# A two-stage kernel on one core: first rows for the MLP by a product with a 0/1 matrix, and the first units in another order

## The chip, the cores and the metric

The kernel runs on one core of one Trainium2 chip. The metric is the time of one execution in microseconds, measured on the device. Before the change three runs took 219.55, 219.83 and 222.78 us, a median of 219.83.

A core has five engines, each with its own instruction queue, that meet only at semaphores: PE (matrix products; PEld in the profile is the loading of its stationary operand), DVE (vector), ACT (scalar functions, copies), POOL and SP (SP here only starts transfers). Sixteen DMA engines move data between HBM and the on-chip memory. Products are accumulated in PSUM, eight banks of 512 f32 numbers for each of 128 partitions, which DVE and ACT must read ("evict") before a bank is used again.

## What is computed

Linear attention on 8 batches of 8 heads, 576 rows of 64, and then a "mixture of depths": in each batch 128 of 576 rows go through an MLP, and the others are passed on.

```python
q_s = exp(q - max(q, -1)); q_s /= sum(q_s, -1) + 1e-9      # over the 64 of a row
k_s = exp(k - max(k, 2));  k_s /= sum(k_s, 2) + 1e-9       # over the 576 rows
kv = einsum('bhsd,bhse->bhde', k_s, v)
x  = einsum('bhsd,bhde->bhse', q_s, kv)                    # heads side by side: (8, 576, 512)
scores = einsum('bsd,d->bs', x, w_gate)
for b in range(8):
    top = argpartition(-scores[b], 128)[:128]
    h = maximum(x[b, top] @ w1, 0)                         # 512 -> 1024
    out[b] = x[b]
    out[b, top] += sigmoid(scores[b, top])[:, None] * (h @ w2)   # 1024 -> 512
```

Everything is f32. Inputs are q, k, v (9.4 MB each), w1 and w2 (2.1 MB each); the output has 9.4 MB.

## The kernel before

**Units.** The attention is cut into 16 units: a batch and four of its eight heads. 576 rows lie on 128 partitions, five (R) on even partitions and four on odd ones, the fifth being padded. For each unit `u` the steps are:

- `load` (L92): k, v, q from HBM, two transfers each, started by SP's queue into one of three sets of buffers (`u % 3`), so a load waits until the unit three before has been read.
- `k_exp` (L193, ACT, one exponential over k), `q_exp` (L198, ACT, in halves `i` = 0 and 1), `v_copy` (L204, v beside a column of ones; by DVE, or by POOL for units 1 to 4).
- `kv_mm` (L207, PE): 20 products that add up `k^T v` with the sums of k in the last column. The trace counts 40, since each f32 product is two instructions. `kv_out` (L219): DVE takes reciprocals (L224), ACT copies kv to `kv_w` (L226), DVE makes a column that holds kv times the gate's weights (L228, L229).
- `q_t` (L231): PE transposes q's exponentials (L239), 10 for each half, and ACT evicts them with a scale (`qT`, L242).
- `x_mm` (L246, PE, L253): x, its sums and its score in one product. `x_out` (L259, DVE): reciprocal (L266), the scaled x into `xs` (L267), the scores of these heads into `sr` (L269). `x_store` (L271): SP writes x to HBM.

**Selection.** After both units of a batch: `score` (L280) sums the heads' scores and splits row numbers and scores into bf16 parts (POOL, L292, L294). `score_row` (L296): PE lays the scores along a row (L302), ACT evicts it in two copies (L305, L307). `compare` (L310, DVE, five times): counts for each row how many come before it, its rank. `pick` (L329): DVE compares ranks with slot numbers to a 0/1 matrix `hit` (L335), a small product on PE (L339) gives each slot its row's number, three reductions and a minimum on DVE (L343 to L345) make the index, and POOL gathers the chosen rows of x from HBM (L347, an indirect DMA into `xr`). `gate` (L352) takes the sigmoid.

**MLP.** `turn` (L362): PE transposes the gathered rows (L368), ACT copies them to `xT` (L370). `mlp1` (L373, L382) and `mlp2` (L388, L392) run in eight pieces each; after pieces 4 and 8 of `mlp1` ACT takes the ReLU (L385). `finish` (L395) scales, adds and scatters the rows by an indirect DMA (L400, L401).

**Order.** `tc.manual_schedule()` (L104): each engine runs its instructions in the order in which the code writes them, and a framework adds the semaphores; what waits holds up all that is behind it on its engine. A PSUM tile name (`tp`, `mm`, `x`) has two buffers, used in turn. Before the first unit PE runs 20 bf16 products on ones (L120). The first loop (L520, s = 0 to 3, `EARLY` = 4) does the first four units with `fill` products between (L502; work for nothing), and in the order of its code the first batch's `score` (s = 1) and `pick` (s = 2). After it come `gate` and `turn` of batch 0 (L567, L568). The second loop (L571, s = 4 to 19) weaves unit s with the MLP of the batch four units back, `pieces(n)` (L577) being the next n pieces: `mlp1` in even s, `mlp2` in odd. In it the next unit's `v_copy`, `k_exp` and `kv_mm` are written in step s (L593, L594, L607), and `turn` of the next batch stands after five of `mlp2`'s pieces that follow `pick` (L597, L610, L621, L623).

Of the kernel before, what the change touches and what calls it, by code (L numbers as in the profile page):

```python
# [8 lines left out]
F32 = mybir.dt.float32  # L9
# [8 lines left out]
def kernel(  # L18
# [36 lines left out]
    UP = 2.0 ** 24  # L55
    TINY = 2.0 ** -126
    NV = 5
    WARM = 20
    assert S == 64 * (R + N2) and D == 64 and DM == H * D and DM == 512 and H % 4 == 0
    assert 1 < capacity < S and KF == 8 and NQ == 2  # L60
    assert B * S <= 32 * 256
# [27 lines left out]
    LD = 3  # L89
    raw = {w: [const.tile([P, 4, R, D], F32, name=f"{w}{n}") for n in range(LD)] for w in "qkv"}  # L90

    def load(u, which, queue=nc.sync):  # L92
        b, qd = units[u]
        for what in which:
            src = {"q": q, "k": k, "v": v}[what]
            t = raw[what][u % LD]
            first = src[b, 4 * qd].offset
            for n, rows in ((1, N2), (0, R)):
                queue.dma_start(
                    out=t[n::2, :, :rows].rearrange("p h r d -> p h (r d)"),  # L100
                    in_=bass.AP(tensor=src.tensor, offset=first + n * R * D,
                                ap=[[9 * D, 64], [SD, 4], [1, rows * D]]))

    ctx.enter_context(tc.manual_schedule())  # L104
    for n in range(LD):
        for what in "kvq":
            (nc.vector if n == 0 else nc.gpsimd).memset(raw[what][n][:, :, N2], 0.0)
    load(0, "k")
    load(0, "v", nc.scalar)
    load(0, "q")  # L110
    load(1, "kvq")
    load(2, "kvq")

    ones_b = const.tile([P, 4 * P], BF16, name="ones_b")
# [1 line left out]
    w_ps = bank("tp", 2)  # L118
    for n in range(WARM):
        nc.tensor.matmul(out=w_ps, lhsT=ones_b[:, :P], rhs=ones_b, start=True, stop=True)  # L120

    wg = const.tile([P, NQ, 2, D], F32, name="wg")
    for h in range(2):
        nc.scalar.dma_start(out=wg[part(h)].rearrange("p a i d -> p (a i) d"),
                            in_=bass.AP(tensor=moe_w_gate.tensor, offset=moe_w_gate.offset + h * D,
                                        ap=[[0, 64], [2 * D, 2 * NQ], [1, D]]))
    warm = const.tile([P, 1], F32, name="warm")
    nc.scalar.activation(out=warm, in_=ones_b[:, :1], func=AF.Exp)
    w1 = const.tile([P, KD, F], F32, name="w1")
# [98 lines left out]
        nc.vector.tensor_mul(prod, kv[:, :, :D], wg[:, qd])  # L228
        nc.vector.reduce_sum(out=kw[:, :, D + 1], in_=prod, axis=AX.X)  # L229

    def q_t(u, i):  # L231

        if i == 0:
            st["qT", u] = at.tile([P, 2, R, 2, D], F32, tag="qT", name="qT")
        qe = st["qe", u] if i == 0 else st.pop(("qe", u))
        t_ps = ps.tile([P, 2, 512], F32, tag="x", name="x", bufs=2)
        for r in range(R):
            for a in range(2):
                nc.tensor.transpose(out=t_ps[:, a, r * 64:(r + 1) * 64],  # L239
                                    in_=qe[part(a), i, r].rearrange("p h d -> p (h d)"),  # L240
                                    identity=ident[part(a), part(a)])
        nc.scalar.activation(out=st["qT", u][:, i].rearrange("p r a c -> p a r c"),  # L242
                             in_=t_ps[:, :, :R * 64].rearrange("p a (r c) -> p a r c", r=R),
                             func=AF.Copy, scale=krec[:, u, i:i + 1])

    def x_mm(u, i):  # L246

# [8 lines left out]

    xs, sr = {}, {}

    def x_out(u, i):  # L259
        b, qd = units[u]  # L260
        if qd == 0 and i == 0:
            xs[b] = xp.tile([P, R, NQ, 2, 2, D], F32, tag="xs", name="xs")
            sr[b] = md.tile([P, NQ * 2, G], F32, tag="sr", name="sr")
        x = st.pop(("x", u, i))[:, :, :R * C].rearrange("p h (r c) -> p h r c", r=R)
        rec = qrec[:, u, i].rearrange("p (h r) -> p h r", h=2)
        nc.vector.reciprocal(out=rec, in_=x[:, :, :, D])  # L266
        nc.vector.tensor_mul(xs[b][:, :, qd, i].rearrange("p r h d -> p h r d"), x[:, :, :, :D],  # L267
                             rec.to_broadcast([P, 2, R, D]))
        nc.vector.tensor_mul(sr[b][:, 2 * qd + i].rearrange("p (h r) -> p h r", h=2), x[:, :, :, D + 1], rec)  # L269

    def x_store(u):  # L271
        b, qd = units[u]
# [20 lines left out]
            if c < NV - 1:  # L293
                nc.gpsimd.tensor_sub(left, raw_s if c == 2 else left, vals[:, b, :, c])  # L294

    def score_row(b):  # L296
        s = st["s", b]
        srow = md.tile([P, RP], F32, tag="srow", name="srow")
        for r0, r1 in ((0, N2), (N2, R)):
            t_ps = bank("tp", 2)  # L300
            for r in range(r0, r1):
                nc.tensor.transpose(out=t_ps[:, (r - r0) * P:(r - r0 + 1) * P],  # L302
                                    in_=s[:, r:r + 1].to_broadcast([P, P]), identity=ident)
            if r0 == 0:
                nc.scalar.copy(out=srow[:, :N2 * P], in_=t_ps)  # L305
            else:
                nc.scalar.copy(out=srow[:, N2 * P:], in_=t_ps[:, :P:2])  # L307
        st["srow", b] = srow
# [20 lines left out]
    def pick(b):  # L329
# [3 lines left out]
        for n, (k0, m) in enumerate(slots):  # L333
# [15 lines left out]
                in_offset=bass.IndirectOffsetOnAxis(ap=idx[:m, :1], axis=0))  # L349
            st["pick", b, n] = xr, no, idx  # L350

    def gate(b, n):  # L352
        m = slots[n][1]
        xr, no, idx = st["pick", b, n]
        g = sl.tile([P, 1], F32, tag="g", name="g")
        nc.scalar.activation(out=g[:m], in_=no[:m, 1:2], func=AF.Exp, scale=-1.0)  # L356
        nc.vector.tensor_scalar_add(g[:m], g[:m], 1.0)  # L357
        nc.vector.reciprocal(out=g[:m], in_=g[:m])  # L358
        st["pick", b, n] = xr, g, idx


    def turn(b, n):  # L362
        m = slots[n][1]
        xr = st["pick", b, n][0]
        xT = sl.tile([P, KD, P], F32, tag="xT", name="xT")
        t_ps = bank("mm", 2)
        for d in range(KD):
            nc.tensor.transpose(out=t_ps[:, d * m:(d + 1) * m], in_=xr[:m, d * P:(d + 1) * P],  # L368
                                identity=ident[:m, :m])
        nc.scalar.copy(out=xT[:, :, :m], in_=t_ps[:, :KD * m].rearrange("p (d c) -> p d c", d=KD))  # L370
        st["xT", b, n] = xT

# [146 lines left out]

    for s in range(EARLY):  # L520
        q_t(s, 0)
        q_t(s, 1)
        k_exp(s + 1)
        v_copy(s + 1, nc.gpsimd)
        fill(2)
        x_mm(s, 0)
        x_mm(s, 1)
        fill(2)
        if s == 2:
            kv_mm(s + 1)  # L530
            q_exp(s + 1, 0)
            fill(3)
            pick(0)
            x_out(s, 0)
            kv_out(s + 1)
            x_out(s, 1)
            x_store(s)
            q_exp(s + 1, 1)
        else:
            x_out(s, 0)  # L540
            x_out(s, 1)
            x_store(s)
            if s == 1:
                score(0)
            kv_mm(s + 1)
            q_exp(s + 1, 0)
            kv_out(s + 1)
            if s == 1:
                score_row(0)
                for r in range(R):  # L550
                    compare(0, r)
            q_exp(s + 1, 1)
            if s == 3:
                score(1)
        fill(2)
        if s == 0:
            load_w1(0)
            load_w1(1)
        elif s == 1:
            load_w1(2)  # L560
            load_w1(3)
            load(4, "kvq")
            load(5, "kvq")
        else:
            load_w2(s - 2)
            load(s + 4, "kvq")
    each(gate, 0)  # L567
    each(turn, 0)  # L568

    number = None  # L570
    for s in range(EARLY, NU + LAG):  # L571

        mlp_b, odd = divmod(s - LAG, 2)
        piece = mlp2 if odd else mlp1
        f_next = 0

        def pieces(n):  # L577
            nonlocal f_next
            for _ in range(n):
                each(piece, mlp_b, f_next)  # L580
                f_next += 1

        here = s < NU
        after = s + 1 < NU
        last = s == NU - 1
        ends = s // 2 if here and odd else None
        compared = s // 2 - 1 if here and not odd else None
        chosen = (s - 3) // 2 if here and odd else B - 1 if s == NU else None
        if here:
            q_t(s, 0)  # L590
            q_t(s, 1)
        if after:
            v_copy(s + 1)  # L593
            k_exp(s + 1)  # L594
        pieces(2)
        if chosen is not None:
            pick(chosen)  # L597
        if here:
            x_mm(s, 0)
            x_mm(s, 1)  # L600
            x_out(s, 0)
            x_out(s, 1)
            x_store(s)
        if last:
            score(ends)
        if after:
            kv_and_exp(s + 1)  # L607
        if s + 4 < NU:
            load(s + 4, "kvq")
        pieces(1)  # L610
        if last:
            compared = ends
        if compared is not None:
            score_row(compared)
            for r in range(R):
                compare(compared, r)
        if chosen is not None:
            each(gate, chosen)
        if ends is not None and not last:
            score(ends)  # L620
        pieces(4)  # L621
        if odd and mlp_b + 1 < B:
            each(turn, mlp_b + 1)  # L623
        pieces(1)
        if odd:
            each(finish, mlp_b)
        if s == NU:
            number = sums_in_range()
# [28 lines left out]
```

## Time and profile before

| | us |
|---|---|
| runs: lowest, median, highest | 219.55, 219.83, 222.78 |
| the profiled execution | 217.89 |
| its span (first to last instruction) | 216.0 |
| PE busy, weight loads | 197.5 (91%), 147.2 (68%) |
| DVE, ACT, POOL busy | 116.2 (54%), 88.6 (41%), 34.4 (16%) |
| first product of the MLP (L382) | 42.64 |
| ranks of batch 0 complete (last L315) | 31.67 |
| PE busy of 0 to 10, 10 to 20, 20 to 30, 30 to 40, 40 to 50 | 7.72, 7.36, 7.56, 7.66, 9.97 |
| DMA share in the same stretches | 0.71, 1.08, 1.07, 1.06, 1.08 |

The profile is one execution, recorded by the hardware. Its page gives busy times, 40 slices of the span with each engine's busy share in tenths, the DMA queues, the chain of work that ended last, and the costliest groups of instructions. The trace answers for single instructions: start, duration, engine, line, what it writes and reads, and in brackets how long its engine sat idle before it and what ended that; "issue" means that the profile shows nothing that the engine waited for. A unit's load is 1.77 MB; between 20 and 80 us the DMA engines move some 375 GB/s. q1 is SP's queue, q10 ACT's, q0 POOL's (gathers and scatters), q8 and q14 bring instructions to the engines.

### The profile page before, as it was taken

To read this page: it belongs to the slowest core of one execution; us is meant where nothing else is said; L and a number is where in the kernel's file an instruction comes from. 1 tells how busy PE (TensorE), PEld (TensorE's weight loads), DVE (VectorE), ACT (ScalarE), POOL (GpSimd) and SP (SyncE) were. 2 spreads that over 40 slices of the span, in tenths; PEclk is the share of its full clock that TensorE was granted. 3 is DMA by queue.
4 is the path that set the end of the run, shared out by engine and by line. 5 is a ranking of instruction groups with operands and counts; after the bars stand their busy time and mean duration, and the time that the engine had idled before them with its cause. 6 is when DMAs were issued, how large, how long until landed. Compare 5 with 4: busy or idle time off the path is not lost. (4 is left out here: it accounts for less than half of the span.)

```text
span 216.0 us, 7090 instructions
## 1 busy us (share of the span) xinstructions
PE 197.5 (91%) x3040; PEld 147.2 (68%) x3040; DVE 116.2 (54%) x359; ACT 88.6 (41%) x146; POOL 34.4 (16%) x78
## 2 busy tenths in 40 slices
PE   5987595999999999999999999999999989999960
PEld 2464462799749975897679776996599548749620
DVE  6552595668726774477626872596358665501010
ACT  2386374763626471746265443536263311211100
POOL 6022402300112012200320023001120112101010
PEclk9999999999999999999999999999999999999996
DMA  5999999999999997958594949421313041101001
GB/s 179 299 356 358 375 398 369 362 392 377 377 384 381 375 344 249 314 157 283 171 320 154 313 133 303 161 82 49 113 52 109 7 156 52 49 3 52 5 5 52
DMA packets 39335, 46.81 MB, mean 217 GB/s; under 512 B 2944, under 2 KB 36736, under 8 KB 39296
## 3 DMA queue, kind: packets, MB, share of 16 engines
q1 hardware_dynamic: 36928, 41.36, 56.4%
q0 software_dynamic: 1280, 4.20, 5.7%
q10 hardware_dynamic: 1088, 0.72, 1.1%
q8 instruction: 26, 0.43, 0.8%
q14 instruction: 13, 0.11, 0.2%
HBM read 34.73 MB, written 11.53 MB: 214 GB/s over the span
## 5 line engine op out<-in xcount | busy, mean ns | idle before, releaser
L382 PE MATMUL mm<-xT,w 128*128 128x128 f32 x512 | 62.1, 278 | 0.0
L382 PEld LDWEIGHTS mm<-xT,w 128*128 128x128 f32 x512 | 58.8, 192 | 2.3 <-ACT xT L370 1.5
L392 PE MATMUL mm<-w,hT 128*128 128x512 f32 x128 | 59.9, 603 | 0.0
L315 DVE SCALAR_TENSOR_TENSOR junk<-srow,s,not_before 128x576 bf16<-128x576 f32 x40 | 32.8, 819 | 8.3 <-ACT srow L307 7.2
L392 PEld LDWEIGHTS mm<-w,hT 128*128 128x128 f32 x128 | 22.5, 190 | 21.2 <-issue 20.4
L267 DVE TENSOR_TENSOR xs<-x,qrec 128x640 f32<-128x640 f32 x32 | 26.4, 825 | 1.1
L242 ACT ACTIVATE qT<-x,krec 128x640 f32<-128x640 f32 x32 | 23.9, 792 | 6.2 <-PE x L239 6.1
L400 DVE SCALAR_TENSOR_TENSOR o<-mm,g,xr 128x512 f32<-128x512 f32 x8 | 6.0, 751 | 37.7 <-PE mm L392 37.7
L202 ACT ACTIVATE qe<-q 128x640 f32<-128x640 f32 x32 | 23.6, 739 | 3.0 <-DMA q<-in_q_dram 2.8
L215 PE MATMUL tp<-v_ones,ke 128*64 128x65 f32 x640 | 22.6, 224 | 2.3 <-issue 2.1
L215 PEld LDWEIGHTS tp<-v_ones,ke 128*64 128x64 f32 x640 | 20.3, 137 | 5.3 <-issue 3.0
L253 PE MATMUL x<-kv_w,qT 64*64 64x66 f32 x1280 | 22.4, 221 | 0.0
L347 POOL DMA_INDIRECT xr<-out_dram,idx x8 | 8.0, 996 | 88.8 <-DVE qrec L266 72.6
L253 PEld LDWEIGHTS x<-kv_w,qT 64*64 64x64 f32 x1280 | 20.2, 134 | 2.6 <-ACT qT L242 0.8
L195 ACT ACTIVATE ke<-k 128x1280 f32<-128x1280 f32 x16 | 20.3, 1270 | 2.8 <-DMA k<-in_k_dram 2.8
L385 ACT ACTIVATE hT<-mm 128x512 f32<-128x512 f32 x16 | 9.5, 596 | 28.7 <-PE mm L382 28.7
L239 PEld LDWEIGHTS x<-ident,qe 64*128 64x128 f32 x320 | 11.7, 139 | 11.6 <-issue 5.0
L239 PE MATMUL x<-ident,qe 64*128 64x64 f32 x320 | 14.5, 229 | 4.9 <-issue 1.4
L266 DVE RECIPROCAL qrec<-x 128x10 f32<-128x10 f32 x32 | 6.9, 215 | 20.7 <-PE x L253 20.7
L401 POOL DMA_INDIRECT out_dram<-o,idx x8 | 10.1, 1269 | 46.8 <-DVE o L400 46.8
L226 ACT COPY kv_w<-tp 128x130 f32<-128x130 f32 x16 | 4.3, 266 | 31.4 <-DVE krec L224 31.4
L370 ACT COPY xT<-mm 128x512 f32<-128x512 f32 x8 | 4.7, 585 | 26.9 <-PE mm L368 26.9
(81 smaller groups left out, 126.0 us busy)
## 6 DMA issues: line engine op xcount, KB each, us to landing
k<-in_k_dram SPq DMA_DIRECT2D x16, 320.0 KB, 7.0
q<-in_q_dram SPq DMA_DIRECT2D x16, 320.0 KB, 6.1
out_dram<-xs SPq DMA_DIRECT2D x16, 320.0 KB, 2.9
v<-in_v_dram SPq DMA_DIRECT2D x15, 320.0 KB, 7.9
k<-in_k_dram SPq DMA_DIRECT2D x16, 256.0 KB, 7.2
q<-in_q_dram SPq DMA_DIRECT2D x16, 256.0 KB, 6.4
out_dram<-xs SPq DMA_DIRECT2D x16, 256.0 KB, 3.2
v<-in_v_dram SPq DMA_DIRECT2D x15, 256.0 KB, 7.7
```

The lines of the kernel that those rows point to most:

```text
L195: nc.scalar.activation(out=ke, in_=raw["k"][u % LD], func=AF.Exp)
L202: nc.scalar.activation(out=st["qe", u][:, i], in_=qr[:, i], func=AF.Exp)
L215: nc.tensor.matmul(out=kv[part(h), i], lhsT=ke[:, 2 * i + h, r], rhs=vo[:, 2 * i + h, r], start=(r == 0), stop=(r == N2))
L239: nc.tensor.transpose(out=t_ps[:, a, r * 64:(r + 1) * 64], in_=qe[part(a), i, r].rearrange("p h d -> p (h d)"), identity=ident[part(a), pa ...
L242: nc.scalar.activation(out=st["qT", u][:, i].rearrange("p r a c -> p a r c"), in_=t_ps[:, :, :R * 64].rearrange("p a (r c) -> p a r c", r= ...
L253: nc.tensor.matmul(out=x[part(c), h, r * C:(r + 1) * C], lhsT=qT[part(h), i, r, c], rhs=kv_w[u % 2][part(h), i], start=True, stop=True)
L267: nc.vector.tensor_mul(xs[b][:, :, qd, i].rearrange("p r h d -> p h r d"), x[:, :, :, :D], rec.to_broadcast([P, 2, R, D]))
L315: nc.vector.scalar_tensor_tensor(junk, st["srow", b], st["s", b][:, r:r + 1], not_before[:, r], op0=OP.subtract, op1=OP.is_ge, accum_out=s ...
L382: nc.tensor.matmul(out=h_ps[:, f % 4 * m:(f % 4 + 1) * m], lhsT=w1[:, d, f * P:(f + 1) * P], rhs=xT[:, d, :m], start=(d == 0), stop=(d == ...
L385: nc.scalar.activation(out=hT[:, f - 3:f + 1, :m], in_=h_ps[:, :4 * m].rearrange("p (f c) -> p f c", f=4), func=AF.Relu)
L392: nc.tensor.matmul(out=st["y", b, n][:m], lhsT=st["hT", b, n][:, f, :m], rhs=w2[:, f], start=(f == 0), stop=(f == KF - 1))
L401: nc.gpsimd.indirect_dma_start(out=out_rows[:(b + 1) * S], out_offset=bass.IndirectOffsetOnAxis(ap=idx[:m, :1], axis=0), in_=o[:m], in_off ...
```

## The change

`select` is new: for batch 0 it makes the 0/1 matrix in f32 from the ranks and multiplies x, which is still on chip in `xs`, by it on PE; the product is the transposed chosen rows, as `turn` makes them from the gathered ones. The copy to `xT`, now in `turned`, is shared with `turn`. `pick(0)` and its gather stay, since `finish` needs the rows and the index, and come later. In units 0 and 1 the second half of q's transposes is evicted by DVE. In unit 1 the score columns (`x_sums`) and `score` stand ahead of the scaling of x (`x_scale`), and the second part of `score_row(0)` uses a bank of `mm`. The loads of w1 come ahead of unit 0's store, w2 between the loads of units 4 and 5. Unit 0's k is loaded over two queues, the gate's weights earlier, and the warm-up has 18 products. Unit 3's `x_mm` moves into the second loop; in its steps 4 and 5 (`late`) four pieces of the MLP, or their like in step 4, come first, and this unit's `k_exp`, `v_copy` and `kv_mm` after them, where they used to stand in the step before.

```diff
-    WARM = 20
+    WARM = 18
...
-    load(0, "k")
-    load(0, "v", nc.scalar)
-    load(0, "q")
+    load(0, "k", (nc.scalar, nc.sync))
+    load(0, "vq")
...
-    def q_t(u, i):
+    def q_t(u, i, on_vector=False):
...
+        if on_vector:
+            nc.vector.tensor_scalar(to, src, krec[:, u, i:i + 1], None, op0=OP.mult)
+        else:
+            nc.scalar.activation(out=to, in_=src, func=AF.Copy, scale=krec[:, u, i:i + 1])
...
+    def x_sums(u, i):
...
         nc.vector.reciprocal(out=rec, in_=x[:, :, :, D])
+        nc.vector.tensor_mul(sr[b][:, 2 * qd + i].rearrange("p (h r) -> p h r", h=2), x[:, :, :, D + 1], rec)
+
+    def x_scale(u, i):
...
         nc.vector.tensor_mul(xs[b][:, :, qd, i].rearrange("p r h d -> p h r d"), x[:, :, :, :D],
                              rec.to_broadcast([P, 2, R, D]))
-        nc.vector.tensor_mul(sr[b][:, 2 * qd + i].rearrange("p (h r) -> p h r", h=2), x[:, :, :, D + 1], rec)
+
+    def x_out(u, i):
+        x_sums(u, i)
+        x_scale(u, i)
...
-            t_ps = bank("tp", 2)
+            t_ps = bank("tp" if r0 == 0 else tag, 2)
...
+    def select(b, n):
+
+        k0, m = slots[n]
+        hit = md.tile([P, R, P], F32, tag="hit_f", name="hit_f", bufs=1)
+        nc.vector.tensor_tensor(out=hit[:, :, :m], in0=slot_no[:, None, k0:k0 + m].to_broadcast([P, R, m]),
+                                in1=st["rank", b].to_broadcast([P, R, m]), op=OP.is_equal)
+        t_ps = bank("mm", 2)
+        rows = xs[b].rearrange("p r a i h d -> p r (a i h d)")
+        for d in range(KD):
+            for r in range(R):
+                nc.tensor.matmul(out=t_ps[:, d * m:(d + 1) * m], lhsT=rows[:, r, d * P:(d + 1) * P],
+                                 rhs=hit[:, r, :m], start=(r == 0), stop=(r == N2))
+        turned(b, n, t_ps)
...
     for s in range(EARLY):
         q_t(s, 0)
-        q_t(s, 1)
-        k_exp(s + 1)
-        v_copy(s + 1, nc.gpsimd)
-        fill(2)
-        x_mm(s, 0)
-        x_mm(s, 1)
-        fill(2)
-        if s == 2:
+        q_t(s, 1, on_vector=s < 2)
+        if s + 1 < EARLY:
+            k_exp(s + 1)
+            v_copy(s + 1, nc.gpsimd)
+            fill(2)
+            x_mm(s, 0)
+            x_mm(s, 1)
+            fill(2)
+        if s == 0:
+            x_out(s, 0)
+            x_out(s, 1)
+            kv_and_exp(s + 1)
+            fill(2)
+            for n in range(KD):
+                load_w1(n)
+            x_store(s)
+        elif s == 1:
+            x_sums(s, 0)
+            x_sums(s, 1)
+            score(0)
+            x_scale(s, 0)
+            x_scale(s, 1)
+            x_store(s)
             kv_mm(s + 1)
             q_exp(s + 1, 0)
+            kv_out(s + 1)
+            score_row(0, "mm")
+            for r in range(R):
+                compare(0, r)
             fill(3)
-            pick(0)
+            q_exp(s + 1, 1)
+            load(4, "kvq")
+            load_w2(0)
+            load_w2(1)
+            load(5, "kvq")
+        elif s == 2:
+            kv_mm(s + 1)
+            q_exp(s + 1, 0)
+            fill(2)
+            each(select, 0)
             x_out(s, 0)
             kv_out(s + 1)
             x_out(s, 1)
             x_store(s)
             q_exp(s + 1, 1)
...
+            load(6, "kvq")
...
-    each(gate, 0)
-    each(turn, 0)
...
+    late = EARLY, EARLY + 1
...
+        if s == EARLY:
+            pieces(1)
+            x_mm(s - 1, 0)
+            x_mm(s - 1, 1)
+            pick(0)
+            x_out(s - 1, 0)
+            x_out(s - 1, 1)
+            x_store(s - 1)
+            score(1)
+            each(gate, 0)
+            pieces(3)
+        elif s in late:
+            pieces(4)
+        if s in late:
+            k_exp(s)
+            v_copy(s)
+            kv_and_exp(s)
+            load(s + 3, "kvq")
+            pieces(1)
+        after = after and s + 1 not in late
...
-        if s + 4 < NU:
+        if after and s + 4 < NU:
             load(s + 4, "kvq")
-        pieces(1)
+        if s not in late:
+            pieces(1)
...
-        pieces(4)
+        if s not in late:
+            pieces(4)
         if odd and mlp_b + 1 < B:
             each(turn, mlp_b + 1)
         pieces(1)
```

## The prediction

> **What bounds the kernel now.** I read the page's slices first, then the timeline from 0 to 64 us.
>
> ```profile
> PE   5987595999999999999999999999999989999960
> DMA  5999999999999997958594949421313041101001
> ```
>
> A slice is 5.4 us. From slice 8 (42 us) PE has hardly a gap until 172 us, and its chain ends the run: each us that PE loses or gains before 42 us, and each that is added after it, moves the end by as much. Up to 80 us the DMA engines are full, but after 42 us PE never waits for a load. So the sum goes by one marker: the start of the second batch's transposes of gathered rows (`turn(1)`, L368). PE has done the same set of work before it in both kernels (but for the first batch's rows), and from there on the programs are alike.
>
> The timeline (start, duration, engine, line, operation; in brackets the idle time and what ended it):
>
> ```profile
> 19.42 0.40 PE L239 MATMUL x<-ident,qe 64*128 64x64 f32 x6 [1.35 <-issue]
> 20.33 1.25 POOL L205 COPY v_ones<-v 128x1280 f32<-128x1280 f32 x1 [5.25 <-DMA v<-in_v_dram]
> ...
> 25.56 0.33 PE L215 MATMUL tp<-v_ones,ke 128*64 128x65 f32 x3 [2.09 <-issue]
> ...
> 25.83 0.65 PE L302 MATMUL tp<-ident,s 128*128 128x128 f32 x4
> ...
> 27.39 0.82 DVE L315 SCALAR_TENSOR_TENSOR junk<-srow,s,not_before 128x576 bf16<-128x576 f32 x1 [0.34 <-ACT srow L307]
> ...
> 30.92 1.52 PE L215 MATMUL tp<-v_ones,ke 128*64 128x65 f32 x40
> ```
> ```profile
> 31.70 0.82 DVE L335 TENSOR_TENSOR hit<-slot_no,rank 128x640 bf16<-128x640 f32 x1
> ...
> 36.62 0.53 PE L239 MATMUL x<-ident,qe 64*128 64x64 f32 x10 [1.13 <-ACT qT L242]
> ...
> 42.64 2.05 PE L382 MATMUL mm<-xT,w 128*128 128x128 f32 x16
> ...
> 44.62 1.40 PE L253 MATMUL x<-kv_w,qT 64*64 64x66 f32 x80
> ...
> 48.81 4.63 PE L382 MATMUL mm<-xT,w 128*128 128x128 f32 x40
> ...
> 53.47 0.60 ACT L385 ACTIVATE hT<-mm 128x512 f32<-128x512 f32 x1 [2.98 <-PE mm L382]
> ...
> 53.83 0.82 DVE L205 COPY v_ones<-v 128x1280 f32<-128x1280 f32 x1
> ...
> 56.90 1.01 POOL L347 DMA_INDIRECT xr<-out_dram,idx  x1 [13.39 <-DVE no L345]
> ```
> ```profile
> 63.12 0.50 PEld L368 LDWEIGHTS mm<-ident,xr 128*128 128x128 f32 x4 [0.52 <-DMA xr<-out_dram,idx]
> ```
>
> The reader is to see: two pauses of PE (1.35 and 2.09 us) that no engine or load ends, the score transposes (L302) right behind the second; the MLP's first product at 42.64; the marker at 63.12. Every engine runs its instructions in the order the code writes them (at 31.7 to 36.9 DVE has pick, x_out, kv_out, x_out, as written), so what stands behind a waiting instruction waits too.
>
> **The change, step by step**, on this execution's clock. PE pitches, start to start: 40 products of kv 1.33 us (45.95 to 47.26), x 1.34, transposes of a unit 0.77 (53.37 to 54.14), an mlp1 piece 8 x 0.117 = 0.93 (4.63/40), an mlp2 piece 0.86 (two of 0.43).
>
> *1. Until the ranks: 0.2 us gained.* x of unit 1 ends at 21.69; with the score columns first the scores stand at about 22.85 (reciprocal 0.21, product 0.16, sum and masks 0.63) instead of 24.05. But their transposes stand behind unit 2's kv products, whose 38th waits until 25.56. The two pauses lie 127 matmuls (254 instructions) apart, and the trace has 16 KB packets on the instruction queue (26 in all on the page) that start at 17.2, 23.2 and 29.3 us, each takes about 1.1 us, and PE goes on 1.1 us or so after its end: PE waits for its code, whose pages come 6.1 us apart while the DMA engines are full. The change moves the page's edge by 4 instructions. So L302 comes as before; its second part saves 0.31 us of waiting for a bank, of which ACT's copies pass on some 0.2. Ranks 31.5, `hit` in f32 0.82 (L267, as many f32 elements, has 0.82) to 32.3. [...]
>
> Evicting unit 0 and 1's second half on DVE costs 0.82 (L267) for ACT's 0.79, in parallel; it lets unit 1's k exponentials start earlier, but kv of units 1 and 2 waits for v to land (POOL's copies at 13.83 and 20.33). Unit 0's k on two queues, `wg` and two warm-up products fewer: unit 0's x hangs on q landing at 10.45, and as many bytes lie ahead of it as before; between 0 and 1 us, I take 0. w1 ahead of the stores changes no byte count ahead of unit 4's load, and w1 is not needed before 40 us: 0. Cover gone, w1's median of 7.6 us from issue (last issued about 24) would still land before that.
>
> *2. The 0/1 product.* PE is free after kv(3) and two fills, at 32.9. 4 x 5 f32 products are 40 instructions in the trace's count (an mlp1 of 32 has 64): at 0.117, 4.7 us, to 37.55. If it went like L368's transposes (4 in 0.60), 20 would take 3.0; same shape and type speak for 4.7. `turn(0)`, 0.60, goes.
>
> *3. Behind it on ACT: a wait of 1.8 us.* The copy xT (0.59) is written ahead of kv_out(3)'s copy, q_exp(3,1) and qT(3,0), which now wait for 37.6: 38.15, 38.4, 39.1, 39.85. The second transposes of unit 3 wait for that qT as at 36.62: PE idles 38.0 to 39.85. Then piece 1, x(3), pick (0.35) and three pieces: 40.3, 41.2, 42.55, 42.9, 45.7.
>
> *4. kv(4): a wait of 1.95 us.* ACT has the ReLU of piece 4 (0.60) and then k_exp(4) (1.27): 47.6, so kv(4) starts at 47.7. On DVE pick's three reductions, x_out(3) twice, score, gate and v_copy(4) come to the same (42.9 + 0.5 + 2.15 + 0.65 + 0.35 + 0.82 = 47.4). Unit 4's data landed by 39.7.
>
> *5. kv(5): a wait of 2.1 us.* PE: kv 1.33, piece 0.93, transposes 0.77, two pieces 1.98, x 1.34, score 0.6, piece 0.93, four mlp2 pieces 3.42: 59.0. DVE: x(4) starts at 52.7, x_out ends 3.1 later (44.62 to 47.72), five compares 4.28 (49.63 to 53.91), and only then v_copy(5) 0.82: 60.9, kv(5) at 61.1.
>
> *6. turn(1): a wait of 1.9 us.* kv 1.33, piece 0.86, transposes 0.77, two pieces 1.72, pick 0.35: 66.1. Then 0.67 to the gather's issue (56.23 to 56.90) and its landing:
>
> ```profile
> DMA to landing us min/median/max: 3.3/3.9/6.2
> ```
>
> The 6.2 are the first two gathers, with the DMA engines at 1.07 of a full share; 3.3 to 4.2 are the rest, at 0.87 and less. With loads 7 and 8 held back by their buffers until 50 and 64 us I take 3.9: 70.7. Before, x(5), kv(6) and five pieces covered it; the pieces now stand earlier, and x and kv (2.7) end at 68.8.
>
> *7. After that nothing is gained back.* SP's store(2) waits for x_out(2,1) at about 40 with load(6) behind it; DMA has some 5 us in hand there, and unit 6 is wanted at 64.
>
> **Sum:** 70.7 against 63.12: +7.5 us. Cross-check: product for turn +4.1, four waits +7.8, less 4.6 of waits (1.21, 1.13, 0.52) and fills (four of 0.43) that PE had between 32.9 and 63.12, makes 7.3. The profiled execution took 217.89 (span 216.0), so 225.4; the median of the runs is 219.83, 1.9 above it, and I forecast 219.83 + 7.5 = **227.3**.
>
> **Rivals.**
> *A, on the other side: the code pages come in time.* Then L302 follows kv(2) as soon as v(2) is copied: 21.58 + 1.33 = 22.9 for 25.83, and everything from step 2 hangs on it. Price: 2.9 us less: +4.6. From 3.1 us on it is not slower by 2%; the first loads' new order (0 to 1 us) can add that: about +3.9, 223.7. For it: scores ready at 22.85. Against it: a page at both edges, and no fewer bytes in flight. 0.15.
> *B, the clock and the gather.* The gather lands in 6.2: +2.3, a PE gap of 4.2 us. At the end the granted clock is 0.53 from 212 to 216 us, after a last matmul at 208.8 that had it at 1.00; the warm-up's first 12 products stand 0.43 apart, until 7.4 us, then about 0.21: 5.1 us at half speed, so up to 2.6 us lost. +9.8 to +12.4, about 231. 0.14. [...]
> *C, faster:* even if none of the four waits came, product and earlier start (+4.1 - 4.6) would leave the time as it is; only that together with A gives over 2%. 0.05.
> Forecast (+5 to +9.7): 0.66.
>
> **How the numbers follow.** 2% (4.4 us) is about what a measurement of this kernel can tell. Slower: forecast 0.66 and B 0.14, less what of the forecast's foot may fall below, 0.78; same 0.16; faster 0.06. The product's lower end (-1.7) and the first loads' (-1) reach to 224.6, A to 223.7; up, the gather and half of the clock's price reach to 231. Range 223.5 to 231.
>
> **What the profile would show.** L302 within 0.5 us of 25.8 (step 1); the 40 products over 4.7 us from 32.9 (2); ACT's kv_w of unit 3 directly behind xT at 38 (3); PE idle before kv(4) ended by ACT ke, before kv(5) by DVE v_ones, before L368 by the gather, each about 2 us (4 to 6); then no PE gap until the last batches. Wrong would be a kv(4) that starts before 45, or the marker before 68.

## The result, and the profile after

The changed kernel takes a median of 226.62 us (four runs, 225.77 to 227.59) beside 219.69 us of the kernel before (four runs): a ratio of 1.033, 95% interval 1.0263 to 1.0397. It is slower by 6.9 us; the prediction was 227.3 us. Ratios compare the executions of each kernel that lie within 1.5% of its fastest. Its profiled execution took 227.59 us with a span of 225.6; that of the kernel before took 217.89 and 216.0.

The page of the changed kernel, its span and slices of 5.6 us (busy tenths of PE, tenths of full TensorE clock granted, DMA):

```profile
span 225.6 us, 7137 instructions
PE   5488869769967999999999999999999979999970
PEclk9958999799999999999999999999999999999998
DMA  5999999999985998594859495930413040201001
```

PE has holes up to slice 12 (73 us) and none until the last batches, where the kernel before had its last one ahead of 42 us. The clock line has two dips that the profile of before does not have.

The timeline of the changed kernel, in the stretch that decides (start, duration, engine, line, operation; in brackets the idle time and what ended it; L214 is kv's product, L255 x, L238 q's transposes, L375 the new product, L413 `mlp1`, L394 `turn`):

```profile
9.70 0.83 DVE L204 COPY v_ones<-v 128x1280 f32<-128x1280 f32 x1 [2.12 <-DMA v<-in_v_dram]
10.68 1.40 PE L214 MATMUL tp<-v_ones,ke 128*64 128x65 f32 x40 [2.97 <-DVE v_ones L204]
14.97 2.48 PE L255 MATMUL x<-kv_w,qT 64*64 64x66 f32 x80
...
25.42 0.65 PE L315 MATMUL tp<-ident,s 128*128 128x128 f32 x4
...
32.88 1.04 PE L214 MATMUL tp<-v_ones,ke 128*64 128x65 f32 x27 [1.63 <-issue]
```
```profile
34.29 4.63 PE L375 MATMUL mm<-hit_f,xs 128*128 128x128 f32 x40
38.96 0.58 ACT L401 COPY xT<-mm 128x512 f32<-128x512 f32 x1 [8.03 <-PE mm L375]
39.44 0.27 ACT L225 COPY kv_w<-tp 128x130 f32<-128x130 f32 x1
41.09 0.53 PE L238 MATMUL x<-ident,qe 64*128 64x64 f32 x10 [1.71 <-ACT qT L246]
42.63 2.48 PE L255 MATMUL x<-kv_w,qT 64*64 64x66 f32 x80
45.20 3.33 PE L413 MATMUL mm<-xT,w 128*128 128x128 f32 x24
50.37 1.39 PE L214 MATMUL tp<-v_ones,ke 128*64 128x65 f32 x40 [1.84 <-ACT ke L194]
63.80 1.39 PE L214 MATMUL tp<-v_ones,ke 128*64 128x65 f32 x40 [1.85 <-DVE v_ones L204]
73.19 0.66 PE L394 MATMUL mm<-ident,xr 128*128 128x128 f32 x4 [1.46 <-DMA xr<-out_dram,idx]
```

The product, and then four idle times of PE, each ended by the engine that the prediction named: 1.71, 1.84, 1.85 and 1.46 us, 6.86 together. The marker, the second batch's transposes, stands at 73.19 (matmul), where the kernel before had 63.26. What lies behind the marker takes 152.4 us of the span, before 152.7: the loss is made before it, all of it.

The same kernel, busy time in stretches of 10 us (columns: PE, PEld, DVE, ACT, POOL, granted clock, DMA share, GB/s):

```profile
10.00:20.00 10.00, 8.26 (x183) 6.60 (x186) 4.40 (x12) 4.22 (x6) 1.25 (x1) 0.66 1.07 356
40.00:50.00 10.00, 7.44 (x127) 6.94 (x127) 5.98 (x21) 3.47 (x6) 2.76 (x6) 0.83 1.07 374
```

The trace's clock records have the TensorE at half clock from 11.9 to 18.8 us and from 42.6 to 46.1; in these x takes 2.48 us and not 1.40. A mean of 0.83 over 10 us is 3.4 us of half clock.

The two profiles lie 9.7 us apart, the medians 6.9. The profile of before has whole clock from its warm-up to its end (mean 0.991 over the span); other executions of the same kernel have spans of 215.7 us at a mean clock of 0.994, 217.5 at 0.991 and 0.978, and 218.3 at 0.974. Half-clock stretches are thus part of the median of before, and not of its profile.

### The profile page after: what moved, and what is told of

Same layout as the page of the kernel before. It is cut to its first block, busy times and chain, and to the rows that moved or that the text cites. A ratio compares the mean times of both kernels' runs of the same rounds, so it can differ in the third digit from the quotient of the medians.

```text
span 225.6 us, 7137 instructions
## 1 busy us (share of the span) xinstructions
PE 201.1 (89%) x3060; PEld 153.2 (68%) x3066; DVE 119.5 (53%) x363; ACT 86.9 (39%) x144; POOL 33.8 (15%) x77
## 5 line engine op out<-in xcount | busy, mean ns | idle before, releaser
L413 PE MATMUL mm<-xT,w 128*128 128x128 f32 x512 | 63.0, 280 | 0.0
L413 PEld LDWEIGHTS mm<-xT,w 128*128 128x128 f32 x512 | 59.3, 193 | 2.2 <-ACT xT L401 1.3
L214 PE MATMUL tp<-v_ones,ke 128*64 128x65 f32 x640 | 22.8, 225 | 8.3 <-DVE v_ones L204 4.8
L214 PEld LDWEIGHTS tp<-v_ones,ke 128*64 128x64 f32 x640 | 20.5, 138 | 12.2 <-issue 9.5
L255 PE MATMUL x<-kv_w,qT 64*64 64x66 f32 x1280 | 24.6, 233 | 0.3
L246 ACT ACTIVATE qT<-x,krec 128x640 f32<-128x640 f32 x30 | 22.4, 792 | 5.6 <-PE x L238 5.6
L431 DVE SCALAR_TENSOR_TENSOR o<-mm,g,xr 128x512 f32<-128x512 f32 x8 | 6.0, 751 | 34.8 <-PE mm L423 34.8
L255 PEld LDWEIGHTS x<-kv_w,qT 64*64 64x64 f32 x1280 | 22.2, 145 | 2.7 <-ACT qT L246 0.9
L238 PEld LDWEIGHTS x<-ident,qe 64*128 64x128 f32 x320 | 12.0, 144 | 9.8 <-ACT xT L401 3.8
L238 PE MATMUL x<-ident,qe 64*128 64x64 f32 x320 | 14.8, 235 | 2.8 <-ACT qT L246 1.7
L432 POOL DMA_INDIRECT out_dram<-o,idx x8 | 10.2, 1272 | 43.9 <-DVE o L431 43.2
```

What stands on the lines that cost most here:

```text
L214: nc.tensor.matmul(out=kv[part(h), i], lhsT=ke[:, 2 * i + h, r], rhs=vo[:, 2 * i + h, r], start=(r == 0), stop=(r == N2))
L238: nc.tensor.transpose(out=t_ps[:, a, r * 64:(r + 1) * 64], in_=qe[part(a), i, r].rearrange("p h d -> p (h d)"), identity=ident[part(a), pa ...
L246: nc.scalar.activation(out=to, in_=src, func=AF.Copy, scale=krec[:, u, i:i + 1])
L255: nc.tensor.matmul(out=x[part(c), h, r * C:(r + 1) * C], lhsT=qT[part(h), i, r, c], rhs=kv_w[u % 2][part(h), i], start=True, stop=True)
L413: nc.tensor.matmul(out=h_ps[:, f % 4 * m:(f % 4 + 1) * m], lhsT=w1[:, d, f * P:(f + 1) * P], rhs=xT[:, d, :m], start=(d == 0), stop=(d == ...
L432: nc.gpsimd.indirect_dma_start(out=out_rows[:(b + 1) * S], out_offset=bass.IndirectOffsetOnAxis(ap=idx[:m, :1], axis=0), in_=o[:m], in_off ...
```

## The experiments

Kernels that ran on one chip share the runs of the kernel before there. On three chips that kernel took 219.4, 219.9 and 220.0 us; on the chip of e11, e12 and e13 it took 223.1 us, so these are compared by ratio and among themselves. `...` marks left-out parts of an edit. Unless said otherwise an edit is made on the changed kernel. "Marker" is the second batch's transposes, 63.26 before and 73.19 after.

### One part undone at a time

**e1: the first loads, the gate's weights and the 20 warm-ups as before.**

```diff
-    WARM = 18
+    WARM = 20
...
-    load(0, "k", (nc.scalar, nc.sync))
-    load(0, "vq")
+    load(0, "k")
+    load(0, "v", (nc.scalar, nc.scalar))
+    load(0, "q")
...
```

> The changed kernel with the first loads, the gate's weights and 20 warm-up products as before. Theory Q (order of the queues: four waits of PE, 1.71, 1.84, 1.85 and 1.46 us in the profile of the changed kernel, and 4.0 us for the product in place of the transposes): the first kv starts near 9.2 us instead of 10.68, the granted clock stays whole between 12 and 19 us, but the four waits stay; the product starts up to 1.2 us earlier (34.1 to 32.9), so the kernel gets 0 to 1.2 us faster. Rival K (the clock at half from 12.2 to 19.0 and 42.9 to 46.3 us and PE's pauses for code are what costs): 2 us or more faster.

Measured: 227.59 us, ratio 1.0349 (1.028 to 1.0419). kv(0) starts at 8.46 and x(0) at 12.92, 2 us earlier than in the changed kernel's profile, but two pauses for code (1.32 and 2.61 us) and half clock (25.7 to 29.1) follow, the product starts at 34.17 and the marker at 72.97. Time won ahead of the ranks is eaten there; the first loads are not where the 7 us are.

**e2: the product and its copy `xT` behind unit 3's `kv_out`, second `q_exp` and first transposes.** (`select` is in three parts from here on: `select_hit` makes the 0/1 matrix, `select` the product, `selected` the copy.)

```diff
-            each(select, 0)
+            each(select_hit, 0)
             x_out(s, 0)
             kv_out(s + 1)
+            q_exp(s + 1, 1)
+            q_t(s + 1, 0)
+            each(select, 0)
...
-            q_exp(s + 1, 1)
```

> The changed kernel with the product and its copy to xT written behind kv_out and the exponentials of unit 3, and the first half of unit 3's transposes ahead of the product. Theory Q: the wait of PE for ACT's qT at 41.1 (1.71 us) goes, x of unit 3 starts near 40.8 instead of 42.63, PE is not idle ahead of it and its clock may stay whole there (2.48 us becomes 1.40): 1.7 to 2.9 us faster; the other three waits stay as long as they are. Rival K: the pause moves to another place, less than 0.7 us.

Measured: 225.35 us, 1.025 (1.0185 to 1.0314). The wait of 1.71 is 0.22, x(3) starts at 41.03; 1.84 and 1.85 stay and the gather's grows to 1.75; half clock comes at 48.8 to 52.2. Marker 71.81.

**e3: unit 4's `k_exp` and `v_copy` ahead of the MLP's first pieces.**

```diff
         if s == EARLY:
+            k_exp(s)
+            v_copy(s)
             pieces(1)
...
```

> The changed kernel with k_exp and v_copy of unit 4 written ahead of the second loop's first pieces. Theory Q: kv of unit 4 follows piece 4 without a wait (1.84 us less), the other waits stay: 1.5 to 1.9 us faster. Rival (unit 4's data or DVE hold kv of unit 4 anyway): below 0.5 us.

Measured: 225.19 us, 1.0233 (1.015 to 1.0316). The timeline of e3 around kv(4):

```profile
43.15 1.40 PE L255 MATMUL x<-kv_w,qT 64*64 64x66 f32 x80
...
44.62 2.92 PE L413 MATMUL mm<-xT,w 128*128 128x128 f32 x24
...
47.47 1.39 PE L214 MATMUL tp<-v_ones,ke 128*64 128x65 f32 x40
```

kv(4) follows without a wait, and x(3) and the 24 products have their times at whole clock (1.40 and 2.92, for 2.48 and 3.33 above). kv(5)'s wait falls to 0.90, the gather's is 1.62, marker 70.39.

**e4: unit 5's `v_copy` and `k_exp` after unit 4's pieces, ahead of x(4) and the compares.**

```diff
...
         pieces(2)
+        if s == EARLY:
+            v_copy(s + 1)
+            k_exp(s + 1)
```

> The changed kernel with v_copy and k_exp of unit 5 written right behind unit 4's two pieces, ahead of unit 4's x and of the five compares, as the kernel before has them. Theory Q (order of the queues): kv of unit 5 follows the fourth mlp2 piece without its wait of 1.85 us; the waits of unit 4's kv (1.84) and of the batch's turn (1.4 to 1.6) stay: the marker 1.85 us earlier than 73.2, the kernel 1.5 to 1.9 us faster. Rival K (the clock and PE's pauses for code decide, the waits are only where the loss shows): below 0.7 us at the marker.

Measured: 227.04 us, 1.0329 (1.0246 to 1.0412): no gain in the median. In the profiled execution (224.2 us) kv(5) starts at 59.34 with no wait and the marker stands at 68.83, 4.4 us earlier than in the changed kernel's profile; the three other executions had lower mean clocks (0.969 to 0.972, the profiled one 0.994).

```profile
47.84 1.39 PE L214 MATMUL tp<-v_ones,ke 128*64 128x65 f32 x40 [1.84 <-ACT ke L194]
...
59.34 1.39 PE L214 MATMUL tp<-v_ones,ke 128*64 128x65 f32 x40
...
68.83 0.66 PE L394 MATMUL mm<-ident,xr 128*128 128x128 f32 x4 [1.58 <-DMA xr<-out_dram,idx]
```

This execution has whole clock from its warm-up to its end and shows the steps of the prediction undisturbed: product 33.26, second transposes of unit 3 at 40.06, kv(4) at 47.84 (forecast 32.9, 39.85, 47.7).

**e5: `pick(1)` and its gather right after unit 5's transposes.**

```diff
             q_t(s, 1)
+        if s == late[1]:
+            pick(chosen)
...
```

> The changed kernel with pick of batch 1 written ahead of unit 6's v_copy and of the two mlp2 pieces, so that its gather starts about 1.7 us earlier. Theory Q: the transposes of batch 1 follow kv of unit 6 without the wait of 1.46 us for the gather; PE may wait 0.3 us for the 0/1 matrix: 1.0 to 1.4 us at the marker. Rival (the gather lands later when it starts earlier, 6 us as in the first two gathers before): nothing gained.

Measured: 225.89 us, 1.0231 (1.0146 to 1.0317). The gather's wait is 0.21 instead of 1.46, with the other three as they were, marker 71.59.

**e6: the edits of e2, e3, e4 and e5 together.**

> The four edits together: copy behind kv_out, unit 4's and unit 5's k_exp and v_copy early, pick of batch 1 early; product, first loads and all else as changed. Theory Q: 1.7 + 1.84 + 1.85 + 1.3 = 6.7 us less at the marker, and 1.1 less where the clock stays whole: 73.2 to between 65.4 and 66.5, against 63.1 before; the kernel within 2% of the one before, some 2 us slower to equal. Rival K: at most 3 us less, the pauses move on.

Measured: 224.11 us, 1.0178 (1.0103 to 1.0252). kv(4) at 45.23 and kv(5) at 57.26 have no wait; then the gather is late again, issued at 61.54 and wanted at 65.3:

```profile
61.54 1.40 POOL L360 DMA_INDIRECT xr<-out_dram,idx  x1 [14.96 <-DVE no L358]
...
67.60 0.66 PE L401 MATMUL mm<-ident,xr 128*128 128x128 f32 x4 [2.26 <-DMA xr<-out_dram,idx]
```

It lands 6 us after its issue; in the changed kernel it took 3.5, issued at 69.69, when the DMA engines were less full (share 0.90 between 60 and 70 us, 1.04 in e6). Four waits of 6.9 us gone bring the median some 3 us, which is nearer to rival K's forecast than to theory Q's: the new wait, pauses for code and half clock (25.9 to 29.3) stand in the way.

### The product against the gather

**e10: the gather and `turn(0)` instead of the product, in the changed kernel's order.**

```diff
-            each(select, 0)
+            pick(0)
...
         if s == EARLY:
+            each(turn, 0)
             pieces(1)
...
-            pick(0)
```

> The changed kernel without the product: batch 0's rows come by the gather and the four transposes again, pick of batch 0 where the kernel before has it, the transposes ahead of the first MLP piece; everything else as changed. Theory Q: the gather lands near 41 (index near 35, 6.2 us), which is where the MLP starts with the product too (41.5), so the product hides what the gather would cost here: within 1 us of the changed kernel, the later three waits stay. Rival P (the product's 4.6 us are lost time): 3 to 4 us faster.

Measured: 232.97 us, 1.0611 (1.0517 to 1.0704): 6 us slower than the change, not equal. The timeline of e10 and its stretch from 40 to 50 us:

```profile
41.81 1.11 PE L394 MATMUL mm<-ident,xr 128*128 128x128 f32 x4 [3.79 <-DMA xr<-out_dram,idx]
...
43.60 2.08 PE L413 MATMUL mm<-xT,w 128*128 128x128 f32 x8 [0.68 <-ACT xT L401]
```
```profile
40.00:50.00 10.00, 7.52 (x111) 6.83 (x112) 2.77 (x11) 0.69 (x2) 0.39 (x2) 0.62 1.07 372
```

The gather was issued at 34.81 and PE idles 3.79 us for it. In the kernel before the same gather, issued at 33.97, had unit 3's x, kv(4) and fillings as cover, which the new order moved away. Around this idle time (38.0 to 41.8) the clock is half for 10.2 us, from 37.4 to 47.7. With this order the product is the better of the two; how much of the 6 us is the clock stays open.

**e8: the kernel before, with only the product put in (right before `pick(0)`; `turn(0)` left out).**

```diff
             fill(3)
+            each(select, 0)
             pick(0)
...
-    each(turn, 0)
```

> The kernel before with one part of the change: the 0/1 product with its copy to xT written right ahead of pick of batch 0, and no transposes of batch 0's gathered rows; all else as before. Theory Q: the product runs from 33 to 37.7, its copy holds back kv_out and the exponentials of unit 3 on ACT as in the changed kernel, kv of unit 4 starts near 42.7 instead of 39.5, the first MLP product near 45.8 instead of 42.64: about 3 us slower at the second batch's transposes and at the end. Rival: the product fits into PE's waits between 33 and 41 us and spares the gather: equal or up to 1 us faster.

Measured: four executions of 223.46, 226.17, 226.94 and 228.99 us beside 219.92; they scatter too widely for a ratio, but all are slower. In the profiled execution the product runs from 34.39 to 39.02, kv(4) starts at 45.24 (before 39.48) and the marker at 71.02. Half clock (27.6 to 31.0) and a code pause of 1.60 at 53.3 go with it. kv(4) is 2.5 us later than expected and the marker, 7.8 us behind that of before, some 5; the run does not tell the product's own length from what pauses and clock made of it.

### Another order around the product

**e11: the product, in the kernel before's order: unit 3's x and kv(4) in the first loop, `xT`'s copy behind unit 3's work, the second loop as before.** (A larger edit; its core:)

```diff
+        else:
+            each(selected, 0)
+            q_t(s, 1)
+            k_exp(s + 1)
+            v_copy(s + 1, nc.gpsimd)
+            x_mm(s, 0)
+            x_mm(s, 1)
...
+            kv_and_exp(s + 1)
```

> The product stays; around it the order is the kernel before's again: the first loop computes all of unit 3 (x(3) too) and kv(4), the second loop starts with score_row(0) of batch 1 where the kernel before had it, and the copy xT stands behind kv_out(3) and q_exp(3,1). Theory Q (the 7 us are the product's 4.1 to 4.6 plus waits and clock that the order around it makes): the waits behind xT, before kv(4), before kv(5) and before turn(1) are all under 0.5 us; second batch's transposes start at 63.12 + 4.6 - 2 (the old wait for the first batch's rows) or about 65 us, between 63.5 and 66; time within 1% of the kernel before (218 to 222). Rival (the product itself costs the time, by the stretch of TensorE that it takes and the half clock that comes with it): marker at 68 or later, as in the run of the product alone, and 3 to 6 us slower than the kernel before.

Measured: 1.0155 (1.0104 to 1.0205), 226.82 beside 223.1 us. The waits behind `xT` and before kv(4) are 0 and 0.43, the gather's is 0, as theory Q has it, but kv(5) waits 1.40 us, x(1) falls into half clock (2.48 us at 20.49), and the marker is at 68.37: the rival's number, and so is the time. Half of the loss came back, and a new wait stood in the way.

**e12: the same with eight fillings fewer ahead of unit 3's kv, the product straight behind the ranks, kv(3) after it, and `pick(0)` after x(3).**

```diff
-            fill(2 if s < 2 else 2)
+            fill(1 if s < 2 else 2)
...
-            fill((2, 2, 2)[s])
+            fill((1, 0, 2)[s])
...
-            fill(2)
+            fill(0)
...
-            fill(3)
+            fill(2)
...
```

> As the run before, but with nine filling matmuls fewer ahead of the second batch-0 score row's last piece, so that the third pause for code on TensorE (before: after 13 products of kv(3)) falls behind score_row(0) of batch 0 and no longer ahead of the product; the product is issued as soon as the ranks are there, right behind score_row, and kv(3) behind it. Theory P (pauses for code sit at a count of matmuls, so what is taken out ahead of the edge brings the ranks forward): score_row at 23 to 24.5 us (25.4 to 26.8 in the runs so far), hit matrix at 29 to 30.5 (31.4), product starts at 29.5 to 31, second batch's transposes at 61 to 63.5; time 216.5 to 218.5, up to 1.5% faster than the kernel before. Rival (the pauses come with time, by when the blocks of instructions arrive, not by the count): score_row no earlier than 25.4, product no earlier than 33, marker 64 or later, time 219 to 222.

Measured: 1.0134 (1.0094 to 1.0174), 226.39 us. The score row stands at 23.60 (e11: 26.09), the hit matrix at 30.30 (31.82), the product at 31.27 (34.31): theory P's numbers, but for 0.3 us at the product, which no longer stands behind kv(3) either. The marker is at 68.85 all the same, where 61 to 63.5 was expected, and later than in e11. The timeline of e12:

```profile
31.27 4.70 PE L379 MATMUL mm<-hit_f,xs 128*128 128x128 f32 x40 [1.83 <-DVE qrec L271]
...
40.63 1.39 PE L214 MATMUL tp<-v_ones,ke 128*64 128x65 f32 x40
...
48.66 0.83 DVE L204 COPY v_ones<-v 128x1280 f32<-128x1280 f32 x1 [3.58 <-DMA v<-in_v_dram]
...
49.63 2.34 PE L214 MATMUL tp<-v_ones,ke 128*64 128x65 f32 x40 [2.36 <-DVE qrec L271]
```

kv(4) stands at 40.63, but kv(5) has to wait for v(5), which lands at 48.66, and half clock (49.8 to 53.2) follows. In the kernel before v(5)'s copy began at 43.39:

```profile
43.39 0.83 DVE L205 COPY v_ones<-v 128x1280 f32<-128x1280 f32 x1 [0.57 <-DMA v<-in_v_dram]
```

Of e11's wait this is the cause too: its copy began at 48.55, when v(5) landed.

**e13: e12's order and fillings, with the gather instead of the product, and kv(3) ahead of `pick(0)`.**

```diff
-            each(select_hit, 0)
+            kv_mm(s + 1)
+            q_exp(s + 1, 0)
+            q_exp(s + 1, 1)
+            pick(0)
...
+            each(turn, 0)
...
```

> The same order and the same fewer fillings, but the first batch's rows come by the gather and four transposes, as in the kernel before, instead of the product: pick(0) behind kv(3), transposes behind x(3). If the gain of the run before is the order's (theory P), this has it too: gather issued at 30 to 31.5, landed 6 us later, second batch's transposes at 61 to 64, time within 1 us of the run before. If the product is what gains there, this run is 2 us or more slower than the run before.

Measured: 1.0348 (1.0288 to 1.0409), 230.72 us, 4.3 us more than e12. The third pause for code falls into kv(3) after 21 of its products, in e11 after 13: eight fillings fewer, eight products later.

```profile
31.53 0.80 PE L214 MATMUL tp<-v_ones,ke 128*64 128x65 f32 x19 [1.85 <-issue]
...
42.16 1.11 PE L401 MATMUL mm<-ident,xr 128*128 128x128 f32 x4 [3.34 <-DMA xr<-out_dram,idx]
```

The gather is issued only at 35.02, lands 7 us later, and the half clock lasts 13.7 us. In this order too the version with the product is 4 us faster than that with the gather, half clock included.

**e14: e12, with w2's two loads back where the kernel before had them (behind unit 5's loads, and behind unit 6's).**

```diff
             load(4, "kvq")
-            load_w2(0)
-            load_w2(1)
             load(5, "kvq")
...
+            load_w2(0)
             load(6, "kvq")
...
+            load_w2(1)
             load(7, "kvq")
```

> The order and fillings of the run with the moved code page's edge, and only the two loads of w2 go back to where the kernel before had them: one behind unit 5's loads, one behind unit 6's. In that run kv(5) waited 2.36 us for v(5), whose copy began when it landed at 48.66 us (43.39 in the kernel before), and the half clock came on behind the wait (kv(5) took 2.34, the score row 1.45). Theory L (w2, 2 x 1 MB, 5.6 us at the 376 GB/s of this stage, stands ahead of unit 5's loads, and so the loads limit whatever TensorE gains): v(5) copied at 43 to 45, kv(5) starts right behind x(5-1) at about 47.3, no half clock at 49 to 53, second batch's transposes at 64 to 66 (68.85), time 3 to 4 us less than that run against its kernel before: ratio 0.99 to 1.003. Rival (all bytes are wanted by then, and the wait only moves to the next unit's loads): kv(5) early, but 2 us or more of waiting for loads at kv(6) or before w2's first product, marker at 67.5 or later, ratio 1.01 or more.

Measured: 220.32 us (twelve runs) beside 219.96 of the kernel before (seventeen): 1.0038 (0.9997 to 1.0078). Only these two loads differ from e12, and the intervals of the two ratios, each to the kernel before on its own chip, do not touch. The timeline of e14:

```profile
46.40 0.83 DVE L204 COPY v_ones<-v 128x1280 f32<-128x1280 f32 x1
...
47.26 1.40 PE L255 MATMUL x<-kv_w,qT 64*64 64x66 f32 x80
...
48.58 1.39 PE L214 MATMUL tp<-v_ones,ke 128*64 128x65 f32 x40
...
66.90 0.60 PE L401 MATMUL mm<-ident,xr 128*128 128x128 f32 x4
```

v(5)'s copy has no transfer to wait for any more, and kv(5) stands right behind x(4), with no half clock after it, although this execution's kv(0) began 1.4 us later than e12's (10.68 and 9.28). The marker is 0.9 us later than expected, and the gain over e12 is some 2 us by the ratios, not 3 to 4. The mechanism of theory L holds: w2's 2.1 MB, 5.6 us at the 376 GB/s that the kernel before moved from 40 to 50 us, stood ahead of unit 5's loads. And since e14 has the product, e11's rival, that the product itself costs the time, falls: with another order around it, and eight fillings fewer, the time is that of the kernel before. No version here beats the kernel before; e14 equals it.

## Why the prediction was right, and where it missed

**Direction, size and mechanism held.** The median rose by 6.9 us for +7.5 forecast, and the profile has the product and the four waits, in the order and with the releasers forecast. Each wait taken alone or with others goes as its step said (e2, e3, e4, e5), so they were named rightly. Taking them away does not return their length: by the ratios the runs give 0 to 2 us for one and 3 us for the four, since the next limit (the gather, a pause for code, the clock) takes over. Only the four together (e6) are clear of the changed kernel's interval; what a single wait is worth rests on the profiles.

That 6.9 is so near 7.5 is partly luck. The sum has no half clock in it, and the marker of the profiled execution went up by 9.9, not 7.6; but that execution lies 1.0 us above the median of its kernel, and the profile of before 1.8 below. The sum itself is confirmed by e4 at whole clock: without kv(5)'s wait of 2.1 us it gives a marker of 68.6, and e4 has 68.83.

*Step 1, until the ranks.* The hit matrix was forecast at 31.5 and stood at 31.44, but by luck. The step took 0 (a gain between 0 and 1 us) for the first loads; v(0) landed later and its copy began at 9.70 instead of 7.50, and kv(0) at 10.68 instead of 9.22. In the eleven profiles with the new first loads kv(0) begins at 9.28 to 10.68, in the three with the old ones at 8.46 to 9.22: these loads cost time there. Half clock from 11.9 to 18.8 came on top. The pauses gave this back: kv(2) ran without one, since its 16 KB of code had landed by 23.8, before kv(2) began at 23.97. That PE pauses for its code holds: e1, where PE is 2 us earlier, has both pauses (1.32 and 2.61 us), and its product starts at 34.17 for 34.29. And in these runs the place goes by a count of instructions: e1, with two warm-up products more than e2, has its pauses after 4 of ten transposes and 37 of kv(2)'s products, e2 after 6 and 39; e13's shift by eight against e11 says the same. The step's times of the three packets are 0.3 us late: on the timeline's clock they start at 16.9, 23.0 and 29.0, 6.1 apart as it says, and PE goes on 1.3 and 1.5 us after the end of the first two. In the changed kernel PE's pause in kv(3) is 1.63 us (DMA share 1.07 from 30 to 40 us); the longest in its variants is the 2.92 us in e3's kv(2) (share 1.03 from 24 to 28).

*Step 2, the product.* Forecast 32.9 to 37.55; measured 34.29 to 38.92. The length of 4.65 us is right (4.63). The start is 1.4 us late: the step had two pauses for code and left out a third, 1.63 us in the middle of kv(3).

*Step 3, the wait behind `xT`:* 1.8 forecast, 1.71 measured.

*Step 4, kv(4):* 1.95 forecast, 1.84 measured, but at 50.37 instead of 47.7. To the 1.2 us from step 2 come 1.5 of half clock between 42.6 and 46.1: x(3) 2.48 for 1.40, and 3.33 for 2.92 in the three pieces behind it. The prediction's sum has no term for the clock at the forecast's own gaps; rival B had priced the clock, but at the gather. That is the term that was missing, and the profiled marker of 73.19 instead of 70.7 is these two, 1.2 and 1.5, less some 0.2, mostly because the gather landed 0.4 sooner.

*Steps 5 and 6:* 2.1 forecast and 1.85 measured; 1.9 and 1.46, as the gather took 3.5 us and not 3.9. *Step 7*, nothing gained back: 152.4 us behind the marker for 152.7.

*A, the code in time.* For kv(2) it came in the changed kernel's profile, but PE was late by then and nothing was won. e12, with fewer fillings, has the score row 2.5 us and the hit matrix 1.5 us earlier than e11, half of the 2.9 that the rival had as its price. *B.* The gather came in time; the clock half came true, at another place. *C*, that even without the waits the time would only be as before, was right in e14, the best version found; that A on top would give over 2%, no run shows.

**What the prediction did not see:** that w2 ahead of unit 5's loads has a price. In the changed kernel it has none, since kv(5) is later than its data anyway (v(5)'s copy, at 62.83, waits for no DMA). It shows as soon as PE comes early: 2.4 us of waiting in e12 and the half clock behind it, some 1% between e12 and e14.

**Still open:** which share of the 6.9 us is half clock. Its stretches fall at other places in each execution (none in e4's profile, 6.8 and 3.4 us in the changed kernel's), so that single profiles can't be subtracted to better than 2 or 3 us (9.7 between the two profiles, 6.9 between the medians), and no run held the clock fixed.

## What to carry to other kernels

A long dependence, here a gather of 6 to 7 us, is worth replacing by work on the bounding engine only where it isn't covered. Here 4.6 us of product replaced a wait that the old order had nearly hidden, and in the new order copies and exponentials queued behind the product cost more; once these were moved, weights loaded ahead of the next unit's data held PE back. When several small waits are removed and little comes back, look for the one limit that stands just behind all of them; here two loads in another place in the queue were worth 1%, as much as the best of the single waits.

## What the runs showed of the hardware

- **The granted clock was half in stretches around short idle times of PE, in some executions and not in others.** In the changed kernel's clock records they last 6.83 and 3.41 us; in the variants, between 8 and 60 us, some 3.4, but for the 10.2 of e10 and the 13.7 of e13. They came in executions with PE idle times of 1.2 to 3 us (e14: 20.8 to 24.2 us, after 0.76 and 1.75), and not in others with the same idle times (e4: 1.71, 1.84 and 1.58, whole clock; the profile of before: 1.35 and 2.09). The longest lie around the longest idle times: 10.2 us with e10's 1.66, 1.13 and 3.79, 13.7 with e13's 1.85, 1.66 and 3.34. Between the warm-up and the changed kernel's first stretch, which starts at 11.9 us, the longest idle time was 2.97 us.
- **Pauses for code sat at a count of instructions** (in kv(3) after 21 products in e13, 13 in e11; in kv(2) after 37 in e1, 39 in e2), so a few filling matmuls taken out moved a pause from ahead of a critical result to behind it: e2 pauses 2.65 us ahead of its score row at 26.32, e13, with eight fillings fewer, has the row at 22.11 and a pause of 1.99 behind it.
- **In these profiles a gather landed later where the DMA engines were fuller:** 3.5 us issued at 69.7 in the changed kernel (share 0.90 from 60 to 70 us), some 6 issued at 61.5 in e6 (1.04), 7.0 issued at 34.8 in e10 (1.07 from 30 to 40).
